# Softcap attention and routed experts in one kernel: a fixed order for all engines, row-split scores, two expert slots

## The chip, the core and the metric

One core of a Trainium2 chip. TensorE (PE in the profile) multiplies, ScalarE (ACT) evaluates tanh and exp, VectorE (DVE) and GpSimd (POOL) do the rest of the element work, SyncE (SP) issues most transfers. The metric is device time in microseconds, the median over runs of the same program.

## What is computed

```python
def _attn_ref(q, k, v, cap):                 # 8 batches, 12 heads, 448 tokens, 64 wide
    scores = q @ k^T / sqrt(64)
    scores = cap * np.tanh(scores / cap)     # cap = 30
    scores = scores - max(scores)
    attn = exp(scores) / (sum(exp(scores)) + 1e-9)
    return attn @ v

def _moe_ref(x, w_gate, wq, wk, wv, wo):     # x: 8 x 448 x 768, 4 experts of 64
    logits = x @ w_gate
    topk = the two largest; w = softmax over those two
    for e in range(4):
        q, k, v = x @ wq[e], x @ wk[e], x @ wv[e]
        a = causal softmax of (q @ k^T / sqrt(64))
        ye = a @ v @ wo[e]
        out += (w of e where e is among the token's two, else 0) * ye
    return out
```

The second stage reads the first stage's output with the heads side by side.

## The kernel before

Stage A runs over 48 pairs of heads (`NP`; six to a batch, `HP`). A pair's scores are held transposed, keys on the 128 partitions. The 448 keys of a head are cut into three chunks of 128 and 64 that remain; the remainders of the two heads share one tile `kt`. The chunks of head 0 and head 1 lie in the upper and lower 64 rows of `kz`, with zeros in the other half, so each of the six score products (and the seventh with `kt`) contracts over all 128 rows. `fill` writes them into tiles `s` of two banks (`ps_score`, two tiles); `tanh` reads each tile (three of 896 elements a row, one of 448), `expo` runs once for each head (1792 and 1344 elements), with no maximum subtracted, since the cap bounds the scores. `a_pv_mm` multiplies by the values with a column of ones beside them, which gives the sum; `a_pv_out` divides, `a_xt` transposes into `xT`. `a_tr` transposes q and k through PE into one bank and VectorE copies them out in five pieces (`qt` twice, `kz` twice, `kt`). The casts to f16 run on GpSimd (`a_cast`), four pairs ahead.

Stage B follows batch by batch, while the next batch's pairs run: `b_v` (values of four experts and the gate's logits), `b_qk` (projections, two experts a half `r`), `b_gate` and `b_gexp` (top two and weights), `b_fill` and `b_exp` (scores and exponentials of each expert, causal: 1024 and 960 elements a half, two halves), `b_pv` for each of four experts, `b_ot`, `b_wo`, `b_out`. GpSimd sets the future positions to zero with 16 `affine_select` a batch. The last batch has no pairs to hide behind; `last_batch` writes out its order.

PSUM has eight banks: four for scores, four (`ps_aux`, tiles `tps`, `pv`, `xtp`, `vps`, ...) shared by all else. The order of each queue is settled when the program is built: ScalarE's list `prog` is written out, and class `Plan` places PE work between the score fills by modelled durations and due times, with VectorE following PE. `slot` issues loads (a pair of pairs each, five stage buffers), and up to three weight loads a pair on GpSimd's queue; outputs leave on SP.

Of the kernel before, what the change touches and what calls it, by code (L numbers as in the profile page):

```python
# [13 lines left out]


class Plan:

    LAT = 0.2

    def __init__(self):
        self.pe = self.dve = self.act = 0.0
        self.done = {}
        self.aux = [0.0] * 4
        self.naux = 0
        self.opened = {}
        self.work = []  # L30

    def ready(self, u):
        t = 0.0
        for d in u["deps"]:
            if d not in self.done:
                return None
            t = max(t, self.done[d])
        if u["aux"] in ("open", "whole"):
            t = max(t, self.aux[self.naux % 4])
        return t  # L40

    def emit(self, u):
        start = max(self.pe, self.ready(u))
        u["fn"]()
        self.pe = start + u["pe"]
        end = self.pe + self.LAT
        if u["dve"]:
            self.dve = max(self.dve, end) + u["dve"]
            end = self.dve + self.LAT
        if u["aux"] in ("open", "whole"):  # L50
            slot = self.naux % 4
            self.naux += 1
            self.aux[slot] = end
            if u["aux"] == "open":
                self.aux[slot] = 1.0e9
                self.opened[u["group"]] = slot
        self.done[u["key"]] = end
        if u["aux"] == "close":
            self.aux[self.opened.pop(u["group"])] = end
            self.done[u["group"]] = end  # L60

    def step(self, until, latest):


        at = {}
        for u in self.work:
            r = self.ready(u)
            if r is not None:
                at[u["key"]] = max(r, self.pe)
        if not at:  # L70
            return False
        first = min(at.values())
        u = min(
            (u for u in self.work if at.get(u["key"], 1.0e9) <= first + 0.05),
            key=lambda u: u["due"],
        )
        if first > until or first + u["pe"] > latest:
            return False
        self.work.remove(u)
        self.emit(u)  # L80
        return True

    def pump(self, until, latest):
        while self.pe < until and self.step(until, latest):
            pass

    def known(self, key):
        return key in self.done or any(key in (u["key"], u["group"]) for u in self.work)

    def force(self, key):  # L90


        def hurry(k):
            for u in self.work:
                if k in (u["key"], u["group"]):
                    u["due"] -= 1.0e6
                    for d in u["deps"]:
                        hurry(d)

        hurry(key)  # L100
        while key not in self.done:
            assert self.step(1.0e9, 1.0e9), key

    def add(self, key, pe, dve, deps, due, fn, *args, aux="whole", group=None):


        self.work.append(
            dict(
                key=key, pe=pe, dve=dve, deps=deps, due=due, fn=lambda: fn(*args), aux=aux,
                group=group,  # L110
            )
        )

    def parts(self, key, n, pe, dve, deps, due, fn, *args):

        for i in range(n):
            d = deps if i == 0 else [(*key, "part", i - 1)]
            aux = "open" if i == 0 else "close" if i == n - 1 else None
            self.add(
                (*key, "part", i), pe / n, dve * (i == n - 1), d, due, fn, *args, i, aux=aux,  # L120
                group=key,
            )
# [3 lines left out]
def kernel(  # L126
# [25 lines left out]
    TL = S - KM  # L152

    WIN = (0, 128, 256, S - 128)

    const = ctx.enter_context(tc.tile_pool(name="const", bufs=1))
    stage = ctx.enter_context(tc.tile_pool(name="stage", bufs=5))
    hd = ctx.enter_context(tc.tile_pool(name="hd", bufs=3))
    actp = ctx.enter_context(tc.tile_pool(name="actp", bufs=3))
    xp = ctx.enter_context(tc.tile_pool(name="xp", bufs=2))  # L160
    bp = ctx.enter_context(tc.tile_pool(name="bp", bufs=2))
    outp = ctx.enter_context(tc.tile_pool(name="outp", bufs=4))
    ps_score = ctx.enter_context(
        tc.tile_pool(name="ps_score", bufs=2, space=bass.MemoryType.PSUM)
    )
    ps_aux = ctx.enter_context(tc.tile_pool(name="ps_aux", bufs=4, space=bass.MemoryType.PSUM))

    ctx.enter_context(tc.manual_schedule())


    staged = {}

    def load(p, n=2):

        if p >= NP:
            return
        b, j = divmod(p, HP)
        h0, h1 = 2 * j, 2 * (j + n)
        e2 = nc.scalar if n == 1 else nc.sync
        qf = stage.tile([QP, 2 * n, QC * Dh], f32, name=f"qf_{p}", tag="qf")  # L180
        kf = stage.tile([128, 2 * n, KC * Dh], f32, name=f"kf_{p}", tag="kf")
        vf = stage.tile([128, 2 * n, KC * Dh], f32, name=f"vf_{p}", tag="vf")
        ktf = stage.tile([128, n, Dh], f32, name=f"ktf_{p}", tag="ktf")
        vtf = stage.tile([128, n, Dh], f32, name=f"vtf_{p}", tag="vtf")

        def tails(dst, src):
            t = src[b, h0:h1, KM:S].rearrange("(j two) p d -> two p j d", two=2)
            nc.sync.dma_start(dst[0:64], t[0])
            e2.dma_start(dst[64:128], t[1])

        e2.dma_start(qf, q[b, h0:h1].rearrange("h (p c) d -> p h (c d)", c=QC))
        nc.sync.dma_start(kf, k[b, h0:h1, 0:KM].rearrange("h (p c) d -> p h (c d)", c=KC))
        tails(ktf, k)
        later = [
            lambda: nc.sync.dma_start(
                vf, v[b, h0:h1, 0:KM].rearrange("h (p c) d -> p h (c d)", c=KC)
            ),
            lambda: tails(vtf, v),
        ]
        if n == 2:  # L200
            for f in later:
                f()
        for i in range(n):
            h = slice(2 * i, 2 * i + 2)
            staged[p + i] = (qf[:, h], kf[:, h], vf[:, h], ktf[:, i], vtf[:, i])
        return later

    LOAD, CAST, TR = 8, 4, 2
    for f in load(0, 1) + load(1, 1):
        f()  # L210


    warm = const.tile([128, 512], f16, name="warm")
    nc.vector.memset(warm, 0.0)
    ident = const.tile([128, 128], f16, name="ident")
    make_identity(nc, ident)
    kz = [const.tile([128, 2, KM], f16, name=f"kz{i}") for i in range(4)]
    ktz = [const.tile([128, 128], f16, name=f"ktz{i}") for i in range(6)]
    for t in (ktz[0], kz[0], ktz[1], kz[1]):
        nc.vector.memset(t, 0.0)  # L220

    def evac(dst, src, act=False):
        (nc.scalar.copy if act else nc.vector.tensor_copy)(dst, src)  # L223


    cast = {}
    vcast = {}

    def a_cast(p, eng=None):
        if p >= NP:  # L230
            return
        eng = nc.gpsimd if eng is None else eng
        if 2 <= p < len(ktz):
            nc.gpsimd.memset(ktz[p], 0.0)
        if 2 <= p < len(kz):
            nc.gpsimd.memset(kz[p], 0.0)
        assert p < 8 or ("pv", p - 8, 1) in plan.done and ("tr", p - 6) in plan.done
        qf, kf, vf, ktf, vtf = staged.pop(p)
        q16 = hd.tile([QP, QC, 2, Dh], f16, name=f"q16_{p}", tag="q16", bufs=6)
        k16 = hd.tile([128, KC, 2, Dh], f16, name=f"k16_{p}", tag="k16", bufs=6)  # L240
        eng.tensor_copy(q16, qf.rearrange("p h (c d) -> p c h d", c=QC))  # L241
        nc.gpsimd.tensor_copy(k16, kf.rearrange("p h (c d) -> p c h d", c=KC))  # L242
        for g in range(2):
            r = slice(64 * g, 64 * (g + 1))
            eng.tensor_copy(ktz[p % 6][r, r], ktf[r, :])
        cast[p] = (q16, k16)
        vcast[p] = (vf, vtf)
        if p > 1:
            a_castv(p)

    def a_castv(p):
        vf, vtf = vcast.pop(p)
        if p < len(v16):
            nc.gpsimd.memset(v16[p][:, :, :, Dh : Dh + 1], 1.0)
            nc.gpsimd.memset(vtz[p], 0.0)
            for g in range(2):
                nc.gpsimd.memset(vtz[p][64 * g : 64 * (g + 1), g, Dh : Dh + 1], 1.0)
# [47 lines left out]
    def fill(p, i):  # L305
        qt, kk, kt = qkt[p]
        if i == 3:
            del qkt[p]
# [23 lines left out]

    xt = {}

    pvs = {}

    def a_pv_mm(p, i, n, heads):

# [632 lines left out]
```

## Time and profile before

| | us |
|---|---|
| median of three runs (340.18 to 342.02) | 341.12 |
| profiled execution: span from first to last instruction, its own time | 341.0 |
| ScalarE busy | 308.4 |
| PE busy (modelled ends) | 280.2 |
| VectorE busy | 251.1 |
| GpSimd busy | 165.2 |

The granted TensorE clock was 0.989 of full speed on average. In rows of groups, the columns are line, engine, operation, output<-input, shapes and count, then busy us and mean ns of one, then idle time of the engine just before and what ended it. In rows of the timeline and of the chain the first two numbers are start and length in us; a merged row ("x2") covers several instructions. In rows of windows, the stretch comes first, its length, then busy us of PE, PE's weight loads, VectorE, ScalarE and GpSimd, each with its count.

### The profile page before, as it was taken

To read this page: it belongs to the slowest core of one execution; us is meant where nothing else is said; L and a number is where in the kernel's file an instruction comes from. 1 tells how busy PE (TensorE), PEld (TensorE's weight loads), DVE (VectorE), ACT (ScalarE), POOL (GpSimd) and SP (SyncE) were. 2 spreads that over 40 slices of the span, in tenths; PEclk is the share of its full clock that TensorE was granted. 3 is DMA by queue.
4 is the path that set the end of the run, shared out by engine and by line. 5 is a ranking of instruction groups with operands and counts; after the bars stand their busy time and mean duration, and the time that the engine had idled before them with its cause. 6 is when DMAs were issued, how large, how long until landed. Compare 5 with 4: busy or idle time off the path is not lost.

```text
span 341.0 us, 8954 instructions
## 1 busy us (share of the span) xinstructions
PE 280.2 (82%) x3295; PEld 190.1 (56%) x3295; DVE 251.1 (74%) x877; ACT 308.4 (90%) x341; POOL 165.2 (48%) x527
## 2 busy tenths in 40 slices
PE   5766669697899789998799879997899789979772
PEld 1344346465457565765576655765576566657441
DVE  2456656378767897869977897889887897788673
ACT  1999999689999999999999999999999999995422
POOL 2889999555806293256707291438506430220130
PEclk9999999799999999999999999999999999999997
DMA  5989999860172915392087606490162001210116
GB/s 160 264 222 244 244 223 241 202 173 3 48 208 72 293 32 171 123 289 71 7 253 211 184 2 187 138 303 24 47 210 72 3 2 46 94 24 2 48 54 226
DMA packets 65148, 46.21 MB, mean 136 GB/s; under 512 B 25872, under 2 KB 61584, under 8 KB 65104
## 3 DMA queue, kind: packets, MB, share of 16 engines
q1 hardware_dynamic: 53712, 43.43, 44.4%
q0 software_dynamic: 10512, 1.58, 7.3%
q10 hardware_dynamic: 880, 0.62, 0.6%
q8 instruction: 26, 0.43, 0.5%
q14 instruction: 18, 0.15, 0.1%
HBM read 36.19 MB, written 11.01 MB: 138 GB/s over the span
## 4 chain that ended last, share of the span: by engine, by line
ACT 85%; PE 6%; DMA 2%; issue 2%; DVE 2%; POOL 1%; ACTq 0%; POOLq 0%
ACT y L323 39%; ACT p L330 37%; ACT pB L540 7%; POOL pB L548 1%; DMA kf<-in_k_dram 1%; PE qkps L469 1%; PE vps L407 1%; PE s L312 1%; DMA out_dram<-ob 1%; PE sB L528 1%; DMA vtf<-in_v_dram 1%; DVE ob L223 1%; PE qps L469 0%; PE pv L351 0%; ACT L223 0%
## 5 line engine op out<-in xcount | busy, mean ns | idle before, releaser
L323 ACT ACTIVATE y<-s 128x896 f16<-128x896 f32 x192 | 152.6, 880 | 1.9 <-PE s L312 1.9
L330 ACT ACTIVATE p<-y 128x1792 f16<-128x1792 f16 x96 | 149.6, 1562 | 0.0
L548 POOL TENSOR_SCALAR_AFFINE_SELECT pB<-pB 128x128 f16<-128x128 f16 (+1 forms) x128 | 31.9, 280 | 142.9 <-ACT pB L540 141.7
L312 PE MATMUL s<-qt,kz 128*128 128x448 f16 x288 | 82.0, 357 | 14.0 <-ACT y L323 6.0
L351 PE MATMUL pv<-v,p 128*128 128x65 f16 x1152 | 66.2, 194 | 1.2 <-ACT p L330 1.0
L351 PEld LDWEIGHTS <-p 128*128 128x128 f16 x1152 | 53.7, 98 | 11.0 <-ACT p L330 2.0
L346 PE MATMUL pv<-vtz,p 128*128 128x130 f16 x192 | 42.0, 220 | 3.1 <-DVE kz L223 3.0
L364 DVE TENSOR_TENSOR xk<-pv,rc 128x256 f16<-128x256 f32 x96 | 40.7, 424 | 3.3
L312 PEld LDWEIGHTS <-kz 128*128 128x128 f16 x288 | 26.2, 98 | 26.4 <-issue 13.1
L223 DVE COPY ob<-wops 128x384 f32<-128x384 f32 (+1 forms) x60 | 33.1, 556 | 9.3 <-PE wops L594 8.5
L540 ACT ACTIVATE pB<-sB 128x1024 f16<-128x1024 f32 (+1 forms) x32 | 31.9, 999 | 2.4 <-PE sB L528 2.4
L223 DVE COPY kz<-tps 64x384 f16<-64x384 f16 x94 | 32.9, 350 | 0.7
L379 PE MATMUL xtp<-perm,xk 128*128 128x128 f16 x144 | 21.0, 223 | 14.4 <-DVE xk L364 14.2
L594 PE MATMUL wops<-wo,oT 128*128 128x384 f16 x128 | 29.8, 325 | 1.7 <-DVE oT L588 1.7
L407 PE MATMUL vps<-wvg,xT 128*128 128x260 f16 (+1 forms) x192 | 30.6, 276 | 0.0
L379 PEld LDWEIGHTS <-xk 128*128 128x128 f16 x192 | 14.6, 98 | 27.3 <-DVE xk L364 19.1
L363 DVE RECIPROCAL rc<-pv 128x4 f32<-128x4 f32 x96 | 17.2, 179 | 16.6 <-PE pv L351 15.4
L241 POOL CAST q<-qf 112x512 f16<-112x512 f32 x46 | 28.2, 613 | 2.0
L289 DVE COPY qt<-tps 128x384 f16<-128x384 f16 x48 | 16.9, 352 | 15.2 <-PE tps L279 14.8
L242 POOL CAST k<-kf 128x384 f16<-128x384 f32 x48 | 24.4, 509 | 5.0 <-DMA kf<-in_k_dram 5.0
L390 DVE COPY xT<-xtp 128x448 f16<-128x448 f16 x48 | 18.6, 388 | 11.2 <-PE xtp L379 10.8
L258 POOL CAST v<-vf 128x384 f16<-128x384 f32 x48 | 24.4, 508 | 3.5 <-DMA vf<-in_v_dram 0.5
(100 smaller groups left out, 500.5 us busy)
## 6 DMA issues: line engine op xcount, KB each, us to landing
qf<-in_q_dram SPq DMA_DIRECT2D x23, 448.0 KB, 5.2
out_dram<-ob SPq DMA_DIRECT2D x24, 384.0 KB, 2.8
kf<-in_k_dram SPq DMA_DIRECT2D x23, 384.0 KB, 5.3
vf<-in_v_dram SPq DMA_DIRECT2D x23, 384.0 KB, 4.6
ktf<-in_k_dram SPq DMA_DIRECT2D x46, 32.0 KB, 4.7
vtf<-in_v_dram SPq DMA_DIRECT2D x46, 32.0 KB, 4.1
out_dram<-ob SPq DMA_DIRECT2D x7, 192.0 KB, 2.8
qf<-in_q_dram ACTq DMA_DIRECT2D x2, 224.0 KB, 4.1
```

The lines of the kernel that those rows point to most:

```text
L223: (nc.scalar.copy if act else nc.vector.tensor_copy)(dst, src)
L312: nc.tensor.matmul(sc[:, o, 0:S], lhsT, qt, start=True, stop=True)
L323: nc.scalar.activation(y[(p, g)][:, 2 * (i % 2) : 2 * (i % 2) + n, :], score.pop((p, i))[:, 0:n, 0:S], AF.Tanh, scale=isc / capf,)
L330: nc.scalar.activation(pt, y.pop((p, g)), AF.Exp, scale=capf)
L346: nc.tensor.matmul(pv[:, n, :, :], pt[:, KC, w : w + 128], vtz[p % 8], start=(n == 0), stop=False, skip_group_check=True,)
L351: nc.tensor.matmul(pv[:, n, g, :], pt[:, c, w : w + 128], v16[p % 8][:, g, c, :], start=False, stop=(c == KC - 1), skip_group_check=True,)
L364: nc.vector.tensor_tensor(xt[p][:, 2 * i : 2 * i + 2, :, :], pv[:, :, :, 0:Dh], rc.broadcast_to((128, 2, 2, Dh)), ALU.mult,)
L379: nc.tensor.transpose(ps[:, 128 * n : 128 * (n + 1)], src(n), first if n < 3 else last)
L407: nc.tensor.matmul(ps, xT[b][:, j, w : w + 128], wvg[:, j, 0:cols], start=(j == 0), stop=(j == NDC - 1),)
L540: nc.scalar.activation(pb[:, o0 : o0 + n], st[b].pop(("sc", r, g))[:, 0:n], AF.Exp, scale=isc)
L548: nc.gpsimd.affine_select(out=blk, in_=blk, compare_op=ALU.is_ge, fill=0.0, base=0, pattern=[[1, n]], channel_multiplier=-1,)
L594: nc.tensor.matmul(ps, st[b]["oT", r][:, w : w + 128], wo2[r][:, f * (D // 2) : (f + 1) * (D // 2)], start=(r == 0), stop=(r == 1),)
```

## The change

All of the program but the launch is rewritten. Every instruction is declared with its engine, an assumed occupancy and latency, what it reads and writes, and its group of one bank; `Graph.solve` then places them one at a time, on all five engines, by readiness and due time, three times over, and emits the order found. ScalarE's tanh and exponentials keep the order in which they are declared.

- Scores: `fill` keeps the two heads of a pair in the two halves of 64 rows, without zeros; the two products of a chunk go to two banks from different rows. Only the remainders use all rows.
- Banks: X has three (chunk 0 of both heads, remainders), Y two (chunks 1 and 2 in turn), three are left for all else (A0 to A2). Groups of the second stage can borrow X banks while they are idle.
- ScalarE: tanh of 1344, 896 and 896 elements, and one exponential of 3136 in place for a pair. Its order is X, first Y, the pair before's exponential, then second Y.
- Second stage of seven batches: two slots (first and second choice of each token) instead of four experts. `b_mask` spreads each slot's 0/1 choice over the 64 columns on GpSimd, PE transposes it, VectorE multiplies it into q; `b_score` accumulates both halves of experts, so each query meets the keys of its expert alone; `b_pv` multiplies by the values of all four experts (260 columns) and the mask with the weight picks one; `b_ot` adds both slots while transposing. The gate ranks experts by pairwise comparison and needs the exponential of one difference a token.
- The last batch keeps four experts, with row-split scores, 512-wide exponentials and its values in two banks.
- `tr` is copied out by one instruction of 960 elements; casts go to rings of three; four stage buffers for loads; weights are loaded from the start on GpSimd's queue; a small exponential draws the table load ahead; the first pair begins with a Y chunk.

```diff
-class Plan:
...
+class Graph:
...
+    def solve(self, banks, lent):
...
-        sc = ps_score.tile([128, 2, 512], f32, name=f"s{i}_{p}", tag="score")
-        for o, (g, c) in enumerate(HALF[i]):
-            lhsT = kt if c == KC else kk[:, g, 128 * c : 128 * (c + 1)]
-            nc.tensor.matmul(sc[:, o, 0:S], lhsT, qt, start=True, stop=True)
+        def heads():
+            for g in range(2):
+                r = slice(64 * g, 64 * (g + 1))
+                nc.tensor.matmul(
+                    dst[:, g, 0:S], qk[t][r, S + 128 * (c + 1) : S + 128 * (c + 2)],
+                    qk[t][r, 0:S], start=True, stop=True,
+                )
...
+        if what == "X":
+            pe(S, lambda: nc.tensor.matmul(
+                X[:, 2, 0:S], qk[t][:, S : S + 128], qk[t][:, 0:S], start=True, stop=True),
+                rd, [("s", bs[2])], name=f"sT_{p}", takes=bs[2:3])
...
+        ACTS[what, p] = act(c_act(S * (b - a)), lambda: nc.scalar.activation(
+            y[:, a:b, :], src[:, 0 : b - a, 0:S], AF.Tanh, scale=isc / capf),
...
+            act(c_act(S * (b - a), False), lambda a=a, b=b: nc.scalar.activation(
+                y[:, a:b, :], y[:, a:b, :], AF.Exp, scale=capf), ks, ks, fixed=True,
+                name=f"e{p}")
...
+        dve(c_dve(S + 512, True),
+            lambda: nc.vector.tensor_copy(qk[t], bank16(g)[:, 0 : S + 512]),
...
+    def b_mask(b, s):
...
+            nc.gpsimd.tensor_copy(
+                mB[s], ms[s][x].rearrange("p n (e o) -> p n e o", o=1).broadcast_to((128, 4, E, Dh))
+            )
...
+            dve(c_dve(S, True), lambda g=g, r=r: nc.vector.tensor_tensor(
+                qm[s][r], qB[x][r], bank16(g)[:, 0:S], ALU.mult),
...
+    H0 = ((0, KC, KM, 64), (64, 0, 0, 128), (192, 1, 128, 128), (320, 2, 256, 128),
+          (448, 2, KM, 64))
+    H1 = ((512, 0, 128, 320), (832, 1, 256, 192))
...
+                    for r in range(2):
+                        nc.tensor.matmul(
+                            ps[:, o % 512 : o % 512 + n], kB[x][r][:, keys(c)],
+                            qm[s][r][:, q0 : q0 + n], start=(r == 0), stop=(r == 1),
+                        )
...
+        act(c_act(1024), lambda: nc.scalar.activation(
+            pb[:, 64:], X[:, 0:2, :].rearrange("p a c -> p (a c)"), AF.Exp, scale=isc),
+            [("s", "X0"), ("s", "X1")], [("pB", pi)], fixed=True, name=f"eB{b}_{s}",
+            frees=("X0", "X1"))
...
+                        nc.tensor.matmul(
+                            bank(g)[:, 0 : E * (Dh + 1)], pB[pi][:, o : o + 128],
+                            vB[x][:, c, :, :], start=(t == 0), stop=(t == len(cs) - 1),
+                        )
...
+            dve(c_dve(E * Dh), lambda g=g, k_=k_, n=n: nc.vector.scalar_tensor_tensor(
+                oB[s][:, n, :, :], view(g)[:, :, 0:Dh], rcb[k_][:, 0, :],
+                mw[s][x][:, n, :].rearrange("p (e o) -> p e o", o=1).broadcast_to((128, E, Dh)),
+                ALU.mult, ALU.mult),
...
+    act(1.3, lambda: nc.scalar.activation(rcb[0], warm[:, 0:4].rearrange("p (n o) -> p n o", o=1),
+                                          AF.Exp), ["warm"], [("rcb", 0)])
+    load(0, 1)
+    load(1, 1)
+    weights()
...
+        order = ("Y1", "X", "Y2") if p == 0 else ("X", "Y1", "Y2")
+        for what in order:
+            if what == "Y2" and p:
+                expo(p - 1)
+                if p in exps:
+                    b_score(*exps[p])
...
+            fill(p, what)
+            tanh(p, what)
...
+    for _ in range(3):
+        G.dues(when)
+        order = G.solve(AUX, XB + YB)
+        when = {o.idx: o.start for o in fixed}
+    for o in order:
+        o.fn()
```

More of the change, by code (lines that the diff above doesn't have):

```diff
@@ L13 @@
 AX = mybir.AxisListType
-class Plan:
-    LAT = 0.2
-    def __init__(self):
[L25 to L62, printed above, removed]
-        at = {}
[L66 to L122, printed above, removed]
@@ L125, with c_pe, c_dve, c_act @@
+def c_pe(n):
+    return max(n / 2400.0 + 0.002, 0.029)
+def c_dve(n, half=False):
+    return n / 1920.0 + 0.064 if half else n / 960.0 + 0.073
+def c_act(n, psum=True):
+    return n / 1200.0 + (0.05 if psum else 0.093)
+def c_pool(n):
+    return n / 1000.0 + 0.07
 @with_exitstack
@@ L208 @@
[L208 to L223, printed above, removed]
@@ L226 @@
[L226 to L242, printed above, removed]
+    LB = B - 1
@@ new lines, with bank, bank16, pe @@
+    for i in range(3):
+        BANK[f"X{i}"] = X[:, i, :]
+    for i in range(2):
+        BANK[f"Y{i}"] = Y[:, i, :]
+    XB = tuple(f"X{i}" for i in range(3))
+    YB = tuple(f"Y{i}" for i in range(2))
+    ANY = AUX + XB + YB
+    def bank(g):
+        return BANK[g.bank]
+    def bank16(g):
+        return BANK[g.bank].bitcast(f16)
+    def pe(n, fn, r=(), w=(), grp=None, due=None, name="", occ=None, takes=()):
+        occ = c_pe(n) if occ is None else occ
+        return G.op("PE", occ, fn, r, w, occ + 0.165, due, grp, name=name, takes=takes)
@@ new lines, with gate @@
+    wo2 = [sb(f"wo2_{r}", [128, D]) for r in range(2)]
+    wvg = sb("wvg", [128, NDC, E * Dh + E])
+    ident = sb("ident", [128, 128])
+    perm = sb("perm", [128, 128])
+    pswap = sb("pswap", [128, 128])
+    swap = sb("swap", [128, 128])
+    warm = sb("warm", [128, 512])
+    tri = sb("tri", [128, 4, E, E], f32)
+    rank0 = sb("rank0", [128, 4, E], f32)
+    rank1 = sb("rank1", [128, 4, E], f32)
+    def gate(nm, shape):
+        return [sb(f"{nm}{i}", shape, f32) for i in range(2)]
+    g_c = gate("g_c", [128, 4, E, E])
@@ new lines @@
+    expo(NP - 1, (("X", "Y1"), ("Y2",)))
+    pv(NP - 1)
+    xt(NP - 1, (ACTS["Y2", NP - 1], 4.0))
+    last(ACTS["Y2", NP - 1], 9.0)
+    for o in G.ops:
+        o.first = o.name[:2] in ("sX", "sY", "sT", "tr", "qk", "k1", "q1", "ge")
+    fixed = [o for o in G.ops if o.eng == "ACT" and o.fixed]
+    when, t = {}, T0
+    for o in fixed:
+        when[o.idx] = t
+        t += o.occ
+    for _ in range(3):
+        G.dues(when)
+        order = G.solve(AUX, XB + YB)
+        when = {o.idx: o.start for o in fixed}
```

1473 lines of the change are left out of this document (840 added, 633 removed).

## The prediction

> **What bounds the kernel now.** I read the page's busy table and chain of waits first, to see which engine the end hangs on, then the costliest groups for the counts, then windows over one stretch of six pairs and over the tail.
>
> ```profile
> span 341.0 us, 8954 instructions
> PE 280.2 (82%) x3295; PEld 190.1 (56%) x3295; DVE 251.1 (74%) x877; ACT 308.4 (90%) x341; POOL 165.2 (48%) x527
> ACT 85%; PE 6%; DMA 2%; issue 2%; DVE 2%; POOL 1%; ACTq 0%; POOLq 0%
> L323 ACT ACTIVATE y<-s 128x896 f16<-128x896 f32 x192 | 152.6, 880 | 1.9 <-PE s L312 1.9
> L330 ACT ACTIVATE p<-y 128x1792 f16<-128x1792 f16 x96 | 149.6, 1562 | 0.0
> 102.20:139.80 37.60, 33.47 (x403) 23.24 (x403) 31.34 (x108) 37.60 (x43) 18.44 (x59) 1.00 0.50 148
> ```
>
> The columns of the last row are PE, PEld, DVE, ACT and POOL busy time, then the granted clock. ScalarE does not rest once in 37.6 us, six pairs plus one batch of the second stage, while PE is busy 33.5 us (89%) and VectorE 31.3 (83%). 85% of the chain is ScalarE. The rest of the span is a start before the first tanh, one stall, and a tail:
>
> ```profile
> 9.73 1.73 ACT L323 ACTIVATE y<-s 128x896 f16<-128x896 f32 x2 [0.26 <-PE s L312]
> 64.22 0.91 PE L469 MATMUL qps<-xT,wq 128*128 128x448 f16 x2 [2.69 <-issue]
> 65.96 0.97 ACT L540 ACTIVATE pB<-sB 128x960 f16<-128x960 f32 x1 [2.39 <-PE sB L528]
> 310.60:317.80 7.20, 7.16 (x101) 5.03 (x102) 4.75 (x15) 1.18 (x2) 0.00 (x0) 1.00 0.01 2
> 317.80:321.80 4.00, 1.63 (x13) 0.93 (x12) 2.78 (x9) 2.12 (x6) 0.00 (x0) 1.00 0.25 98
> 321.80:326.00 4.20, 4.09 (x44) 3.27 (x44) 1.90 (x10) 4.16 (x6) 2.96 (x13) 1.00 0.00 0
> 326.00:336.00 10.00, 6.15 (x65) 3.67 (x62) 8.56 (x24) 1.80 (x4) 0.98 (x4) 1.00 0.35 122
> 336.00:341.00 5.00, 0.00 (x0) 0.00 (x0) 0.00 (x0) 0.00 (x0) 0.00 (x0) 0.62 0.68 233
> ```
>
> **The tanh and exp of the pairs.** Durations overlap their neighbours, so starts are what counts:
>
> ```profile
> 33.06 1.33 ACT L330 ACTIVATE p<-y 128x1344 f16<-128x1344 f16 x1
> 34.27 1.36 ACT L323 ACTIVATE y<-s 128x896 f16<-128x896 f32 x2
> 35.52 1.70 ACT L330 ACTIVATE p<-y 128x1792 f16<-128x1792 f16 x1
> 37.10 1.73 ACT L323 ACTIVATE y<-s 128x896 f16<-128x896 f32 x2
> 38.70 1.35 ACT L330 ACTIVATE p<-y 128x1344 f16<-128x1344 f16 x1
> ```
>
> A pair takes 38.70 - 33.06 = 5.64 us. The exponentials start 1.21 and 1.58 us ahead of what follows, so 448 elements cost 0.37 us (0.83 ns each) and a start 0.09. Two tanh of 896 take 1.60, so a tanh start costs about 0.06. The elements of a pair stay (7 x 448). One of four tanh starts and one of two exp starts go: 0.15 us a pair, 48 pairs, **-7.2 us**; a pair becomes 5.49.
>
> **The second stage's exponentials.** A batch had four (1024 and 960 wide), it gets two of 1024:
>
> ```profile
> 61.32 1.04 ACT L540 ACTIVATE pB<-sB 128x1024 f16<-128x1024 f32 x1
> 62.24 1.33 ACT L330 ACTIVATE p<-y 128x1344 f16<-128x1344 f16 x1
> ```
>
> One of 1024 occupies 0.92 us, one of 960 by the slope 0.87. 3.58 becomes 1.84, 1.74 saved in each of the seven batches ahead of the last, **-12.2 us**. Six pairs with a batch then need 6 x 5.49 + 1.84 + 0.1 (gate) = 34.9 us of ScalarE; the same sum for the kernel before gives 37.5, where the window shows 37.6.
>
> **Whether PE still fits.**
>
> ```profile
> 38.54 0.54 PE L312 MATMUL s<-qt,kz 128*128 128x448 f16 x2
> L312 PE MATMUL s<-qt,kz 128*128 128x448 f16 x288 | 82.0, 357 | 14.0 <-ACT y L323 6.0 <-ACT pB L540 3.1 <-ACT kz L223 2.4
> 59.87 0.49 PE L407 MATMUL vps<-wvg,xT 128*128 128x260 f16 x3
> 59.45 0.33 PE L279 MATMUL tps<-ident,k 128*128 128x128 f16 x3
> ```
>
> Two scores of 448 columns take 0.54 and one is recorded as 0.35, so they follow each other by 0.19 us, 0.42 ns a column (transposes of 128 and products of 260 fit that). A pair had seven; it now has three couples (each head in its own 64 rows, its own bank) and one full one. If the two of a couple run together, that is four slots, 3 x 0.19 x 6 = -3.4 us a batch; if one after the other, 0. No row shows such a couple. I take together, as they share neither operand rows nor banks, and keep both ends. Per batch the second stage adds, by columns: 16 mask transposes of 128 (+0.9), 20 products of 260 columns for 40 of 65 (+0.9), 16 instead of 8 transposes of outputs (+0.4), scores 4096 columns for 3968 (+0.1): +2.3. PE comes to 33.5 - 3.4 + 2.3 = 32.4 of 34.9, 93%, against 89% that left ScalarE no idle time. The waits are roomier too: two-bank scores were refilled under one tanh (0.80); now the first Y is refilled under the X tanh (0.83 x 1344 + 0.06 = 1.18) and the second under the 2.7 us exponential.
>
> **VectorE and GpSimd.**
>
> ```profile
> L223 DVE COPY kz<-tps 64x384 f16<-64x384 f16 x94 | 32.9, 350 | 0.7
> L390 DVE COPY xT<-xtp 128x448 f16<-128x448 f16 x48 | 18.6, 388 | 11.2 <-PE xtp L379 10.8
> L289 DVE COPY qt<-tps 128x384 f16<-128x384 f16 x48 | 16.9, 352 | 15.2 <-PE tps L279 14.8
> L293 DVE COPY qt<-tps 128x64 f16<-128x64 f16 x48 | 8.6, 180 | 0.0
> L296 DVE COPY kt<-tps 128x128 f16<-128x128 f16 x48 | 9.9, 206 | 1.9 <-ACT kz L223 1.9
> ```
>
> Five copies (352 + 180 + 2 x 350 + 206 = 1438 ns) become one of 960 elements, by the slope from 128 to 448 about 680: -4.6 us a batch. The batch part grows: 16 gate operations for 9 (+1.3, by the 180 ns of the smallest copy), four mask products (+1.6 by the 388 ns of the copy of that size, up to twice that), eight scaled outputs for four (+1.6 likewise), less 1.5 for four copies of second-stage keys that go. Together about -1.6, up to nothing: 30 to 31 of 34.9 us, 85 to 90% (83% before). It stays hidden, with less cover. GpSimd drops no pair casts, trades 16 masks a batch for four and gains two spreads of 1024; at 18.4 us it has room.
>
> **What the new order adds on ScalarE.** Two waits. The X banks are lent to the second stage: after its exponential the next X scores must be written under one tanh, 0.80 us, and a couple needs 0.19 to issue, 0.35 to land and two handovers of up to 0.26 (the idle time ahead of the first tanh above): 0 to 0.4 over, 0.2 taken, 14 times, +2.8. And the gate's exponential, fixed in ScalarE's order, waits for eleven small VectorE steps where it waited for the logits alone: at about 0.2 us a step 0 to 2.2, seven times; it stands where the planner expects them done, so I take 0.5, +3.5. Behind it on ScalarE stand the tanh, and behind those PE's refills. **+6.3 us** (0 to 15).
>
> **The stall at 62 us.** PE waited 2.69 us ahead of the first `wq` product of the second half.
>
> ```profile
> kf<-in_k_dram SPq DMA_DIRECT2D x23, 384.0 KB, 5.3
> ...
> wq<-in_moe_wq_dram POOLq DMA_DIRECT2D x4, 96.0 KB, 12.2
> q0 software_dynamic: 10512, 1.58, 7.3%
> ```
>
> That queue's loads land 12.2 us after issue in the median. They are now issued at the start instead of three a pair, so ScalarE's 2.39 us go: **-2.4** (0 to -2.8). In return seven of them stand on GpSimd's queue ahead of the first cast of pair 2, and their packets (7.3% of 341 us, 25 us of all 16 engines for 17 loads, 1.5 a load) share the DMA with the loads of pairs 0 to 3. On SP the stores now stand between the loads, and one that waits for its copy holds those behind it; as the stage holds eight pairs and the casts run three ahead, a load has five pairs, 27 us, for its 5.3 to land. I cost that at nothing; a store over 20 us late would uncover it.
>
> **The start.**
>
> ```profile
> 6.94 1.28 ACT L223 ACT_TABLE_LOAD   x1 [6.94 <-DMA vtf<-in_v_dram]
> 8.24 0.47 ACT L223 COPY kz<-tps 64x384 f16<-64x384 f16 x1
> ```
>
> The table load (1.28, on the path) is drawn ahead by a dummy exponential, and one copy of keys replaces two of 0.47, so the first tanh comes near 9.73 - 1.28 - 0.47 = 8.0. But PE's queue has the transposes of pair 2 ahead of the X scores of pair 1; pair 2 must have landed by about 9.5, and its loads share the DMA with the weights: 0 to 3 us late. Net -1.5 to +1.5, **-0.5** taken.
>
> **The tail.**
>
> ```profile
> 327.47 0.43 DVE osc L578
> 327.95 0.41 PE otp L379 x4
> 328.38 0.40 DVE oT L588
> ...
> 329.33 0.32 PE pvB L570 x10
> ```
> ```profile
> 332.99 2.12 PE L594 MATMUL wops<-wo,oT 128*128 128x384 f16 x12 [1.51 <-DVE oT L588]
> ```
>
> Before, by the windows, PE works 7.2 us on end (projections of the last batch that lagged), then come 4.0 of evacuations in turn, 4.2 of exponentials, 10 to the last copy, 5.0 to the end. The new order leaves PE some 20 slots of 0.19 (projections, four output products) behind the last exponential, 3.8; the values' 24 products of 256 (0.11 each, 2.6), under which the evacuations run; eight exponentials of 512 (8 x 0.49 = 3.9); one pass of products, scaling, transposes and copies (0.32 + 0.43 + 0.41 + 0.40, a second scaling and the small steps: 2.6); 2.9 for the output products as before, from 332.99 to 335.9; and 5.0: together 20.8 against 30.4. PE may arrive 1 to 2 us behind. **-8** (-5 to -9.5).
>
> **Sum**, against the profiled execution's 341.0 (the median of three is 341.12): 341.0 - 7.2 - 12.2 + 6.3 - 2.4 - 0.5 - 8 = **317.0 us**.
>
> **The rivals.**
>
> *PE becomes the bound.* The array empties when it passes between 64-row and full products: six passages a pair, each between 0 and the 0.16 us by which a record outlasts the spacing (0.35 - 0.19). At 0.08 a batch gains 2.9 us, PE needs 35.3, just over ScalarE's 34.9; at 0.16, 38.3, seven times 3.4 more. For it: PE is at 93% in my sum. Against: records overlap, so 93% overstates, and the order places other work around the couples. Time 322 to 341, 330 in the middle. The Trainium skill, "TensorEngine Tiling (Array Packing)", section "Key Properties", states this rule: changing the tiling mode drains TensorE. No row here has a mode change, so the trace neither bears it out nor denies it.
>
> *Three work banks instead of four, and one fixed order for all engines.* VectorE, near 87%, frees banks late, PE waits for them, and fills come late: 0.2 us a pair, 10 us in all. For it: VectorE's share grows while the banks that hide its delays shrink. Against: the idle score banks are lent out, and the transposed pairs run up to four ahead. 327.
>
> *Slower: the couples run one after the other and each passage empties the array.* 32.4 + 3.4 + 2.9 to 5.9 = 38.7 to 41.7 us of PE per batch, PE is late in each refill, 7 x 3.8 or more: 317 + 27 = 344, up to 365. It outweighs all the gains once PE needs over 34.9 + 24/7 = 38.3 us a batch. Against: it takes both prices near their upper ends. The Trainium skill, "TensorE: Matmul & The Clock Gate", Part 3, says products in distinct row groups run at the same time; by it this rival falls back to the first. Nothing in this trace shows it.
>
> **How the numbers follow.** Forecast 0.58 (its own range 309 to 324); PE as the bound 0.16, of which 0.03 ends within 0.5% of before; banks and order 0.12; slower 0.14. So faster by over 0.5% 0.83, within 0.5% (about what a measurement of this kernel can tell from none) 0.03, slower 0.14. The low end is all gains at their bounds without waits, near 309; the high end, 333, takes in the second rival and the lower half of the first and leaves the slower one out.
>
> **What would show it.** ScalarE without idle time over six pairs, about 35 us a batch; 144 tanh, 49 pair exponentials, 14 of the second stage; the two score products of a couple starting within 0.02 us; PE near 32 us a batch; no wait at the first `wq` product; first tanh near 8 us; some 22 us behind the last exponential. Wrong if ScalarE waits for X or Y scores more than 0.2 us a pair, if the couples start 0.19 apart, or if score products follow others with 0.1 us or more of silence.

## The result, and the profile after

The changed kernel takes 337.09 us (median of 20 runs, 336.0 to 340.42) against 340.24 us of the kernel before (338.99 to 342.52): a ratio of 0.9913, with an interval of 0.9891 to 0.9935. Faster by a little under 1%; the forecast was 317.0. The profiled execution spans 334.4 us, against 341.0 before, and the reading below goes by it: 17.4 us are missing. (The 341.0 is a long execution of the kernel before: those measured beside the experiments span 336.5 to 340.9. So the difference of the two spans overstates the gain, and the ratio is what counts for that.)

The page of the changed kernel, its busy table, its chain of waits and the groups that answer to those of before:

```profile
span 334.4 us, 8992 instructions
PE 293.5 (88%) x3435; PEld 193.5 (58%) x3435; DVE 239.2 (72%) x752; ACT 291.7 (87%) x232; POOL 160.6 (48%) x451
PE 56%; DVE 17%; POOL 7%; DMA 6%; issue 5%; ACT 5%; SPq 1%; ACTq 0%; DVEq 0%; POOLq 0%
L587 ACT ACTIVATE yp<-yp 128x3136 f16<-128x3136 f16 (+2 forms) x49 | 135.7, 2772 | 0.0
L577 ACT ACTIVATE yp<-Y 128x896 f16<-128x896 f32 x96 | 88.8, 925 | 10.0 <-PE Y L555 9.2
L577 ACT ACTIVATE yp<-X 128x1344 f16<-128x1344 f32 x48 | 62.5, 1302 | 3.7 <-PE X L555 2.2
```

The counts are as announced (96 + 48 tanh, 49 exponentials of pairs), and ScalarE is busy 291.7 us for 308.4. But the chain, 85% ScalarE before, is now 56% PE and 5% ScalarE. Windows of the changed kernel, first over six pairs with one batch of the second stage, then over the tail (columns as in the prediction's windows, and behind the granted clock the share of the DMA engines and GB/s):

```profile
136.74:173.66 36.92, 34.97 (x433) 23.94 (x430) 29.98 (x95) 35.39 (x29) 18.02 (x49) 1.00 0.54 151
309.25:314.70 5.45, 5.45 (x67) 3.71 (x66) 3.94 (x11) 0.00 (x0) 0.00 (x0) 1.00 0.20 75
314.70:319.24 4.54, 3.20 (x35) 2.42 (x34) 3.33 (x13) 1.07 (x3) 0.00 (x0) 1.00 0.22 87
319.24:324.30 5.06, 3.53 (x54) 1.95 (x53) 4.24 (x19) 4.31 (x9) 2.96 (x8) 1.00 0.29 97
324.30:330.45 6.15, 4.15 (x36) 2.28 (x33) 4.63 (x14) 1.92 (x5) 0.00 (x0) 1.00 0.33 112
330.45:334.40 3.95, 0.00 (x0) 0.00 (x0) 0.00 (x0) 0.00 (x0) 0.00 (x0) 1.00 0.65 203
```

PE is busy 35.0 us in a batch where the forecast had 32.4. PE's timeline in the changed kernel (start, duration, line, operation, how many) shows what a couple costs:

```profile
139.48 0.36 PE L555 MATMUL Y<-qk 64*128 64x448 f16 x2
139.68 0.35 PE L555 MATMUL X<-qk 64*128 64x448 f16 x2
139.96 0.50 PE L903 MATMUL A<-wo,oT 128*128 128x384 f16 x2
...
142.56 0.34 PE L607 MATMUL A<-v,yp 128*128 128x65 f16 x6
142.83 0.36 PE L555 MATMUL Y<-qk 64*128 64x448 f16 x2
143.12 0.23 PE L600 MATMUL A<-vtz,yp 128*128 128x130 f16 x1
143.19 0.35 PE L607 MATMUL A<-v,yp 128*128 128x65 f16 x6
143.38 0.22 PE L600 MATMUL A<-vtz,yp 128*128 128x130 f16 x1
```

The two products of a couple are one row of 0.36 us, as long as a single one: they run together. Two couples side by side start 0.20 apart. But the full product behind a couple starts 0.28 or 0.29 after it, 0.09 more; and ahead of the couple, where six products of 65 columns take 0.19 (143.19 to 143.38) and so end at 142.75, PE starts nothing until 142.83. The same shows in the whole trace: from a full product of 448 columns to the next full one it is 0.19 us, to a couple behind it 0.285 in the median, and from a couple to a full product 0.29. A lone couple therefore holds PE for 0.19 + 2 x 0.09 = 0.37 us, which is what two full products cost (0.38). With 139 stretches of split products in PE's order, of 144 couples, that is 139 x 0.18 = 25 us of PE in the whole span.

ScalarE's waits in the changed kernel (engine and line, what it waited for, us in total, times, longest):

```profile
ACT yp L577 <- PE Y L555: 9.2, 16, 2.0
...
ACT g_e L731 <- DVE g_e L726: 4.2, 6, 1.3
...
ACT yp L577 <- PE X L555: 2.2, 4, 0.8
```

### The profile page after: what moved, and what is told of

Read it like the earlier page. It is cut to its first block, busy times and chain, and to the rows that moved or that the text cites. A ratio compares the mean times of both kernels' runs of the same rounds, so it can differ in the third digit from the quotient of the medians.

```text
span 334.4 us, 8992 instructions
## 1 busy us (share of the span) xinstructions
PE 293.5 (88%) x3435; PEld 193.5 (58%) x3435; DVE 239.2 (72%) x752; ACT 291.7 (87%) x232; POOL 160.6 (48%) x451
## 4 chain that ended last, share of the span: by engine, by line
PE 56%; DVE 17%; POOL 7%; DMA 6%; issue 5%; ACT 5%; SPq 1%; ACTq 0%; DVEq 0%; POOLq 0%
PE A L607 7%; PE A L686 7%; PE A L662 6%; PE Y L555 5%; PE A L903 5%; PE A L600 4%; DVE oB L865 3%; PE A L641 3%; DMA ktf<-in_k_dram 3%; PE X L792 3%; PE X L564 3%; PE A L850 2%; ACT yp L577 2%; PE X L555 2%; DVE oT L888 2%
## 5 line engine op out<-in xcount | busy, mean ns | idle before, releaser
L587 ACT ACTIVATE yp<-yp 128x3136 f16<-128x3136 f16 (+2 forms) x49 | 135.7, 2772 | 0.0
L577 ACT ACTIVATE yp<-Y 128x896 f16<-128x896 f32 x96 | 88.8, 925 | 10.0 <-PE Y L555 9.2
L577 ACT ACTIVATE yp<-X 128x1344 f16<-128x1344 f32 x48 | 62.5, 1302 | 3.7 <-PE X L555 2.2
L607 PE MATMUL A<-v,yp 128*128 128x65 f16 x1152 | 58.1, 197 | 0.0
L607 PEld LDWEIGHTS <-yp 128*128 128x128 f16 x1152 | 51.7, 100 | 4.6 <-issue 3.0
L600 PE MATMUL A<-vtz,yp 128*128 128x130 f16 x192 | 43.2, 226 | 6.6 <-ACT yp L587 3.0
L629 DVE TENSOR_TENSOR xk<-A,rca 128x256 f16<-128x256 f32 x96 | 40.5, 423 | 2.7
L544 DVE COPY qk<-A 128x960 f16<-128x960 f16 x47 | 29.6, 650 | 11.7 <-PE A L513 11.4
L555 PE MATMUL Y<-qk 64*128 64x448 f16 x192 | 36.2, 373 | 0.7 <-ACT yp L577 0.5
L912 DVE COPY ob<-A 128x384 f32<-128x384 f32 (+1 forms) x55 | 29.3, 552 | 3.2 <-PE A L903 2.4
L600 PEld LDWEIGHTS <-yp 128*128 128x128 f16 x192 | 18.9, 99 | 15.2 <-issue 9.3
L523 PE MATMUL A<-ident,k 128*128 128x128 f16 x144 | 16.9, 229 | 10.5 <-POOL k L485 7.1
```

The source lines that it names most:

```text
L544: lambda: nc.vector.tensor_copy(qk[t], bank16(g)[:, 0 : S + 512]),
L555: nc.tensor.matmul(dst[:, g, 0:S], qk[t][r, S + 128 * (c + 1) : S + 128 * (c + 2)], qk[t][r, 0:S], start=True, stop=True,)
L577: ACTS[what, p] = act(c_act(S * (b - a)), lambda: nc.scalar.activation(y[:, a:b, :], src[:, 0 : b - a, 0:S], AF.Tanh, scale=isc / capf), [ ...
L587: act(c_act(S * (b - a), False), lambda a=a, b=b: nc.scalar.activation(y[:, a:b, :], y[:, a:b, :], AF.Exp, scale=capf), ks, ks, fixed=True ...
L600: nc.tensor.matmul(ps[:, n, :, :], y[:, 2, w : w + 128], vtz[u], start=(n == 0), stop=False, skip_group_check=True,)
L607: nc.tensor.matmul(ps[:, n, h, :], y[:, SLOT[c][h], w : w + 128], v16[u][:, h, c, :], start=False, stop=(c == 2), skip_group_check=True,)
```

## Experiments

Theory P: passages between split and full products cost about 0.09 us each and make PE the bound. Rival O: a couple costs its 0.19, and the time is lost to the order and to the three work banks.

**Undo the split, or half of a couple.** The three edits are in the loop that sends a couple:

```diff
# e1_two_full
-                r = slice(64 * g, 64 * (g + 1))
+                r = slice(0, 128)
# e2_one_full (e3_one_half keeps r as it was)
-            for g in range(2):
-                r = slice(64 * g, 64 * (g + 1))
+            one = what != "X" and p >= 2
+            for g in range(1 if one else 2):
+                r = slice(0, 128) if one else slice(64 * g, 64 * (g + 1))
```

> The changed kernel with both products of each couple over all 128 rows, so no passage between 64-row and full products is left; the two heads' scores are summed, the output is not the reference's. Theory P (passages): a couple now holds PE for 0.19 + 2 x 0.09 = 0.37 us, two full products for 0.38: time unchanged within 1% (334 to 339 us), PE busy near 293 us, no silence ahead of the score products. Rival O (couples cost 0.19 as forecast; the lost time comes from the order and the three work banks): 18 couples a batch cost 0.19 more each, 3.4 us a batch, 24 us in all: near 360 us.

> The changed kernel with each Y couple (12 a batch, from pair 2 on) cut to one product over all 128 rows; the second Y bank keeps old scores, the output is not the reference's. The X couples stay split. Theory P: PE loses 12 x 0.18 = 2.2 us a batch, and as PE sets the pace the pairs speed up until ScalarE's 35.3 us a batch bind: 11 us less or somewhat more, 322 to 328 us, ScalarE's waits for Y scores (9.2 us) mostly gone. Rival O: less than 3 us gained, 333 to 337 us.

> As e2_one_full, but the one product left of each Y couple is over 64 rows, so both passages stay and only the second product goes; the second head's scores of the Y banks are left out. Theory P: the two products of a couple do run together and the price is that of the passages: time as the changed kernel's, 333 to 339 us. Rival (the second product of a couple costs PE a slot of its own): like e2_one_full, 322 to 328 us.

Measured: e1 335.93 us, ratio to before 0.9906 (0.9876 to 0.9937), the changed kernel's own; e2 329.43, 0.9712 (0.9688 to 0.9736); e3 336.97, 0.9946 (0.9914 to 0.9978). The same place in PE's timeline, of e1, e3 and e2 in turn:

```profile
142.56 0.54 PE L555 MATMUL Y<-qk 128*128 128x448 f16 x2
142.93 0.22 PE L600 MATMUL A<-vtz,yp 128*128 128x130 f16 x1
```
```profile
142.08 0.36 PE L556 MATMUL Y<-qk 64*128 64x448 f16 x1
142.37 0.23 PE L601 MATMUL A<-vtz,yp 128*128 128x130 f16 x1
```
```profile
139.13 0.35 PE L556 MATMUL Y<-qk 128*128 128x448 f16 x1
139.32 0.22 PE L601 MATMUL A<-vtz,yp 128*128 128x130 f16 x1
```

Two full products hold PE for 0.37, one split product alone for 0.29 and the silence ahead of it, one full product for 0.19. The second product of a couple is free, the passages are not, and splitting the rows gained PE nothing. Rival O's 360 us for e1 is out. e2 gained 7.5 us by the spans (326.9 against 334.4) where 11 or somewhat more were expected; its span lies in the 322 to 328 us named, its median above. ScalarE's waits for Y scores fell from 9.2 us to 6.3, of which 4.6 stand in the first six pairs. The smaller gain says that passages aren't all.

**The planner's prices.** e4 tells the planner of passages, e7 gives a lone couple its measured price and moves other numbers of the plan.

```diff
# e4_plan_state
+PASS = 0.09
...
+        def cross(o):
+            return PASS if o.eng == "PE" and split(o) != was[0] else 0.0
...
-            return t
+            return t + cross(o)
...
-    ... occ=0.22, name=f"s{what}_{p}"
+    ... occ=0.19, name=f"s{what}_{p}"
# e7_replan
-                    d = u.due if u.first else max(u.due, t0 + 0.8)
+                    d = u.due if u.first else max(u.due, t0 + 0.4)
...
-    ... u.due < t + o.occ + 0.6 and t2 < t + min(o.occ, 0.25) ...
+    ... u.due < t + o.occ + 0.4 and t2 < t + min(o.occ, 0.15) ...
...
-    ... occ=0.22, name=f"s{what}_{p}"
+    ... occ=0.37, name=f"s{what}_{p}"
...
-    ... due=(ref, 7.0 + 1.4 * n)
+    ... due=(ref, 10.0 + 1.4 * n)
...
-    ... due=(ref, 12.0 + 3.6 * r + ...)
+    ... due=(ref, 16.0 + 3.6 * r + ...)
...
-            [(b, "m1"), (b, "m2")], ["e"])
+            [(b, "m1"), (b, "m2")], ["e"], lat=0.9)
```

> The full computation. Only the planner's idea of PE changes: a couple costs 0.19, and 0.09 more stands wherever PE goes from split to full products or back, so the planner sets couples side by side where it can: 117 episodes of split products instead of 139. Theory P: 22 x 0.18 = 4 us of PE go, and the plan's times come nearer to the chip's: 329 to 334 us. Rival O: 335 to 339 us, unchanged.

> The full computation. Only numbers of the planner change: a couple 0.37 for 0.22, the gate's last step 0.9 us late for 0.2, second-stage products due 3 to 4 us later, closer look-ahead. Theory P with an order made on wrong prices: PE's work stays, but the score products stand where they are needed and ScalarE's waits for Y, X and second-stage scores (about 14 us) fall by 5 or more: 327 to 331 us. Rival: any other order loses as much elsewhere, as in e4_plan_state: 334 to 341 us.

Measured: e4 342.56 us, 1.0115 (1.0081 to 1.015), slower than both kernels and outside both ranges expected; e7 331.07, 0.974 (0.9703 to 0.9777), by its span of 328.8 what theory P expected. e4 has fewer passages and loses far more in single places. ScalarE and PE in e4 at one of them:

```profile
202.02 2.93 ACT L597 ACTIVATE yp<-yp 128x3136 f16<-128x3136 f16 x1
207.56 0.92 ACT L587 ACTIVATE yp<-Y 128x896 f16<-128x896 f32 x1 [2.60 <-PE Y L565]
```
```profile
204.38 1.05 PE L672 MATMUL A<-wvg,xT 128*128 128x260 f16 x8
...
207.15 0.36 PE L565 MATMUL Y<-qk 64*128 64x448 f16 x2
```

The exponential ends at 204.95, but the second stage's value products and other work stand ahead of the Y couple in PE's order, which is sent at 207.15. So the order does matter, in both directions: part of rival O holds beside P. And right prices alone don't make a good order: e4's 0.19 and two passages of 0.09 are what a lone couple was measured to cost. That both changes are needed shows in the next run.

**Both together.**

```diff
# e10_replan_one: e7_replan, with the loop of e2_one_full
```

> The kernel of e7_replan, same order, with each Y couple from pair 2 on cut to one product over 128 rows (second head's Y scores left out, as in e2_one_full). Under the better order a batch takes 36.3 us where ScalarE's own work is 35. If passages are what is left, PE's 2.2 us a batch bring it to 35 to 35.5 us and the time to 321 to 325 us. If e7_replan is held by its order and no longer by PE's work, 326 to 329 us.

Measured: 324.36 us, 0.953 (0.949 to 0.9571), span 322.1. The X tanh of pairs 6 and 42 (six batches apart), as ScalarE's timeline has them in the changed kernel, e2, e7 and e10:

```profile
42.95 1.32 ACT L577 ACTIVATE yp<-X 128x1344 f16<-128x1344 f32 x1
...
267.13 1.34 ACT L577 ACTIVATE yp<-X 128x1344 f16<-128x1344 f32 x1
```
```profile
42.92 1.35 ACT L578 ACTIVATE yp<-X 128x1344 f16<-128x1344 f32 x1
...
260.42 1.34 ACT L578 ACTIVATE yp<-X 128x1344 f16<-128x1344 f32 x1
```
```profile
44.56 1.32 ACT L577 ACTIVATE yp<-X 128x1344 f16<-128x1344 f32 x1
...
262.13 1.32 ACT L577 ACTIVATE yp<-X 128x1344 f16<-128x1344 f32 x1
```
```profile
44.14 1.32 ACT L578 ACTIVATE yp<-X 128x1344 f16<-128x1344 f32 x1
...
255.02 1.33 ACT L578 ACTIVATE yp<-X 128x1344 f16<-128x1344 f32 x1
```

A sixth of each difference is the length of a batch:

| us per batch | order of the change | order of e7 |
|---|---|---|
| all couples split | 37.36 | 36.26 |
| Y couples one full product | 36.25 | 35.15 |

The two changes add: 1.1 us a batch each. With both, a batch stands at 35.15, beside the 34.9 forecast for ScalarE alone. What in e7's order gains its 1.1 is only in part known: between the two tanh, ScalarE's waits for the gate's exponential go from 3.0 us to none and those for Y scores from 4.4 to 1.1, while those for second-stage scores rise from 0.5 to 3.0; which of the plan's numbers did it was not separated. The window of e10 over one batch shows the bound back on ScalarE, which does not rest in it, nor in four of the six batches between the two tanh:

```profile
143.06:177.97 34.91, 33.07 (x417) 23.76 (x416) 29.60 (x95) 34.91 (x29) 18.13 (x48) 1.00 0.57 159
```

Over the whole span, start and tail included, e10's chain still has 50% PE and 21% ScalarE.

**The gate's exponential.** In the gate, the largest logit is taken off first and the last step becomes a maximum:

```diff
# e5_gate
...
+            g_l[x], lg[x], g_m1[x].broadcast_to((128, 4, E)), ALU.subtract),
...
-    ... g_l[x], ms[0][x], -1.0e30, lg[x], ALU.mult, ALU.add
+    ... g_l[x], ms[0][x], -1.0e30, g_l[x], ALU.mult, ALU.add
...
-        g_(lambda: V.reduce_max(g_m2[x], g_l[x], axis=AX.X), ...
-        g_(lambda: V.tensor_tensor(g_e[x], g_m2[x], g_m1[x], ALU.subtract), ...
+        g_(lambda: V.reduce_max(g_e[x], g_l[x], axis=AX.X), ...
```

> The full computation. The gate takes the largest logit off ahead of the ranks and ends in a maximum, so that no small VectorE operation with two operands in SBUF is left between the masks (which start GpSimd's 1024-element spread) and the gate's exponential. Theory L: the 4-element subtraction took 0.53 to 0.85 us in five of seven batches because it ended with the spread that ran beside it; with it gone ScalarE's waits ahead of the gate's exponential fall from 4.2 us to under 1. Rival: VectorE's backlog is what is late, and the 4.2 us stay. For the time, theory P (PE sets the pace) lets at most 2 us of that come through: 332 to 335 us in the profiled execution; if ScalarE set the pace, 330 to 331.

Measured: 336.41 us, 0.9905 (0.987 to 0.9939): no change that can be told. VectorE beside GpSimd in the changed kernel, then in e5:

```profile
172.57 0.17 DVE L725 TENSOR_REDUCE g_m<-g_l 128x4 f32<-128x16 f32 x1
172.78 0.74 DVE L726 TENSOR_TENSOR g_e<-g_m,g_m 128x4 f32<-128x4 f32 x1
```
```profile
172.46 2.03 POOL L753 CAST mB<-ms 128x1024 f16<-128x1024 f32 x2 [2.50 <-DVE ms L720]
```
```profile
172.83 0.17 DVE L728 TENSOR_REDUCE g_e<-g_l 128x4 f32<-128x16 f32 x1
```
```profile
172.72 2.03 POOL L754 CAST mB<-ms 128x1024 f16<-128x1024 f32 x2 [2.50 <-DVE ms L720]
```

The subtraction ends at 173.52, when the first of the two spreads ends (172.46 + 1.04); the maximum in e5 runs beside a spread in 0.17. The mechanism of theory L is seen, but not what it was to explain: ScalarE still waited 3.8 us for the gate, where theory L had less than 1, so the rival holds. The wait most likely comes from where the exponential stands in ScalarE's order, too early for a VectorE that runs late: in e7, where the plan counts on 0.9 us for that step, the wait is gone with the old gate, though e7 moves other numbers too.

**The weight loads.** e6 issues them behind the casts of pair 3; e11 is e7 with them spread over the pairs 1 to 11.

```diff
# e6_weights_late
-    gp(0.85, lambda: nc.gpsimd.dma_start(dst, src), w=[key], ...
+    gp(0.85, lambda: nc.gpsimd.dma_start(dst, src), [("q16", 3 % NQ16)], [key], ...
...
     load(1, 1)
-    weights()
...
         cast(p)
+        if p == 3:
+            weights()
# e11_replan_spread
+        AT = [1, 1, 2, 2, 3, 3, 4, 4, 5, 5, 6, 6, 6, 8, 9, 10, 11]
...
+            if AT.pop(0) == p:
...
+        weights(p)
```

> The full computation. The 17 weight loads are issued behind the casts of pair 3 instead of at the start. Theory S: their packets hold back the loads of pairs 0 to 3, which cost the first batch ScalarE waits of 3.7 us behind the first tanh: these fall under 1.5, and the time to 331 to 333 us. Rival: those loads fill the DMA engines by themselves, or the stall comes back at the first products with the weights near 45 to 62 us: 334 to 338 us.

> The full computation: the kernel of e7_replan, with the same order on PE, and the weight loads spread out, one to three with the casts of each of the pairs 1 to 11 instead of all at the start. Theory S: ScalarE's waits in the first 46 us (e7_replan: 7.3 us) shrink by 2 us or more without a stall behind it: 325 to 327 us. Rival: the DMA engines are full for 45 us either way, and what is gained at the first pairs is lost at the next, as in e6_weights_late: 328 to 330 us.

Measured: e6 337.48 us, 0.9935 (0.9895 to 0.9975); e11 330.76, 0.9717 (0.9664 to 0.9771), which can't be told from e7. Theory S was half right, and the times are what its rivals expected (e11's by its span of 328.3). In e6 ScalarE's waits in the first 24 us shrink (0.32 and 0.66 us behind the first tanh, where the changed kernel had 0.59, 2.00 and 0.83) and come back 20 us later, on its timeline:

```profile
19.31 0.92 ACT L577 ACTIVATE yp<-Y 128x896 f16<-128x896 f32 x1 [0.66 <-PE Y L555]
41.27 0.92 ACT L577 ACTIVATE yp<-Y 128x896 f16<-128x896 f32 x1 [1.66 <-PE Y L555]
44.75 0.92 ACT L577 ACTIVATE yp<-Y 128x896 f16<-128x896 f32 x1 [1.39 <-PE Y L555]
```
```profile
34.63 0.52 POOL L455 DMA_DIRECT2D wo<-in_moe_wo_dram  x1 [1.45 <-DMA wq<-in_moe_wq_dram]
```

The second fence is GpSimd in e6: issuing a load, it waits, by the profile, for an earlier one of its own queue to land, and the casts of the next pairs stand behind it. That is not all of it: PE starts nothing in the 1.8 us before 33.99, and in the windows from 34 to 44 us its granted clock is 0.50 to 0.52, where a couple's row is 0.56 us long for 0.36. How much of the two stalls is the clock's wasn't separated.

**Versions with everything.** e8 is e5's gate, e6's loads and e4's planner with later due times and another look-ahead; e9 is e5's gate and a planner that knows passages too, with other numbers (couple 0.22, passage 0.06) and without the late loads; e12 is e5's gate and prices near e7's, and sends a pair's second Y couple together with the next pair's X couple.

```diff
# e12_merged
+            def both():
+                heads()
+                for g in range(2):
+                    r = slice(64 * g, 64 * (g + 1))
+                    nc.tensor.matmul(X[:, g, 0:S], qk[u][r, S + 128 : S + 256], qk[u][r, 0:S], ...
```

> The full computation: the gate of e5_gate, the late weight loads of e6_weights_late, and a planner that knows a couple as 0.19 and each passage as 0.09 with the later due times. 114 episodes of split products for 139, 4.5 us less of PE. If the parts add up: 323 to 328 us. If the order decides by chance, as in e4_plan_state: 333 to 340 us.

> The full computation: the gate of e5_gate, the weights loaded at the start as in the changed kernel, and a planner that counts each passage (a couple 0.22, a passage 0.06) with second-stage products due later: 115 episodes of split products. e8_all lost 5.4 us in one stall at 42 us behind its late weights; without it theory P gives 327 to 330 us. If setting couples side by side is no use, as e4_plan_state could be read, 332 us or more.

> The full computation: the gate of e5_gate, and the second Y couple of a pair sent as one operation with the X couple of the next pair (33 times, wherever no second-stage scores stand between), so that 110 episodes of split products are left of 139; prices in the planner as in e7_replan (a lone couple 0.40, a double one 0.50). Theory P: against e7_replan 28 x 0.18 = 5 us less of PE's work; if half of it comes through, 326 to 329 us. If, as in e9_aware_gate, the new order gives back what the passages save: 330 to 334 us.

Measured: e8 333.46 us, 0.9822 (0.9779 to 0.9865); e9 331.96, 0.9752 (0.9703 to 0.98); e12 330.32, 0.9721 (0.9661 to 0.9781). By their medians all three missed what theory P gave for them, e12 narrowly: e8 and e12 lie in their rival's range, e9 just below it (e12's span, 327.5, would be theory P's). Their 110 to 115 stretches of split products instead of 139 save 4 to 5 us of PE, yet e9 and e12 end where e7 ends with 138, and e8 above it: what setting couples side by side brings wasn't separated from what the new order costs. Between the X tanh of pairs 6 and 42, e12's batches take 35.71 us each (45.06 to 259.29), 0.56 less than e7's, and the rest of its span gives 2 of these 3.3 us back; e8's and e9's batches, 36.5 and 36.6, are no shorter than e7's. The fastest versions that compute everything are e7, e11 and e12, at 0.972 to 0.974 of the kernel before and below the changed kernel's interval; e9, at 0.975, can't be told from them.

## Why the prediction was wrong

Of the 17.4 us between 317.0 and 334.4, 9.4 lie between the X tanh of pairs 6 and 42 (224.2 us, where six batches of 34.9 and 0.9 of waits make 214.8), 3.0 at the start, 2.8 in the tail, and what is left, 2.2, by subtraction on the last six pairs, where ScalarE waits 3.6 us for 0.9 counted.

- **ScalarE's savings: right.** A pair that waits for nothing takes 5.47 us (forecast 5.49), a second-stage exponential 0.91 (0.92), and four of e10's batches, at 34.86 to 34.96 with ScalarE busy throughout, are the forecast 34.9.
- **PE: the step that failed.** "I take together" was right, and "That is four slots, 3 x 0.19 x 6 = -3.4 us a batch" was not: a couple costs 0.37 with its passages, so -3.4 became about 0, and PE had 35.0 us of work a batch for 32.4 (the couples alone would make it 35.8, so its other terms came out 0.8 smaller together). The first rival named this mechanism, its price within 0.01 us, PE's 35.3 and a range of 322 to 341, and got a chance of 0.16. By its own rule, though, 0.09 a passage makes 32.4 + 36 x 0.09 = 35.6 us of PE and a time near 322: that 334.4 lies in its range is in part luck. The row for a passage was missing, and the sum took it at zero although the bound was 0 to 0.16 six times a pair. Of its own signs of being wrong, the silence of 0.09 stayed just under the 0.1 it named, and the waits for X and Y scores behind the first tanh (10.3 us over 48 pairs, 0.21 a pair) just passed its 0.2. The Trainium skill, "TensorEngine Tiling (Array Packing)", section "Key Properties", has TensorE drain at a change of tiling mode: the trace agrees, 0.09 us each way. The Trainium skill, "TensorE: Matmul & The Clock Gate", Part 3, has products in distinct row groups run at the same time: e3 agrees.
- **The new waits: the two that it named came out, a third was put at nothing.** +6.3 us was taken, 0.9 a batch. The gate's exponential waits 4.2 us for 3.5, and X scores behind a second-stage exponential 2.2 for 2.8. But "The waits are roomier too" failed: between the X tanh of pairs 6 and 42 ScalarE waits 4.4 us for Y scores, 10 times out of 12 for a first Y couple behind an X tanh. In all a batch is 37.36 there where ScalarE needs 34.8, so 2.6. e2, e7 and e10 divide it: 1.1 for the Y couples' passages, 1.1 for the order, 0.35 left. "The order places other work around the couples" was the argument against the first rival; with two engines at 35 us of work each, the order's share came out as large as that of the Y couples' passages.
- **The stall at 62 us: right.** No wait stands ahead of a `wq` product there.
- **The start: mis-sized.** The first tanh comes at 8.52 (forecast 8.0), but ScalarE then waits 3.7 us in the first six pairs where 1.2 was counted. e6 moves these waits rather than removing them.
- **The tail: mis-sized.** 25.2 us instead of 22.4 (30.4 - 8), by the windows: PE works 5.4 us behind the last exponential (3.8 and 1 to 2 late), evacuations with the values' products take 4.5 (2.6), the exponentials 5.1 (3.9), and the 10.1 behind them agree with 10.5.
- **Banks (the second rival):** not tried alone; e10 keeps the three banks, and only 0.35 us a batch is left there. **The slower rival** needed couples that run in turn, and e3 shows that they don't.
- **Slips in the sums** that decide nothing: 20 products of 260 columns for 40 of 65 are +1.1 us by columns, not +0.9; the terms named for the lent X banks reach 0.26 over, not 0.4; and the upper bounds of the two waits, 0.4 x 14 and 2.2 x 7, make 21, not 15.

## What to carry to other kernels

A row split saves TensorE time only if the passages are few beside the split products: here two 64-row products with full ones on both sides cost as much as two full products. When a change takes work off the bounding engine and leaves a second one within a tenth of it, the next bound is the question, and an unpriced cost on that second engine must enter the forecast at its middle and not at zero. With two engines near the bound, the order of the work is a cost of its own: another order of the same work (e7, with other prices, due times and look-ahead) was worth as much as the Y couples' passages. Measured prices alone didn't find it: e4 had them and was slower than both kernels.

## What the runs showed of the hardware

A passage between 64-row and full products costs PE 0.09 us each way. A VectorE subtraction of four elements with both operands in SBUF takes 0.16 us where no cast runs (in the last batch) and up to 0.85 beside a GpSimd cast, ending when the cast does, while a maximum with one operand takes 0.16 to 0.17 beside the same casts (e5). The Trainium skill, "SBUF — State Buffer", section "Who interferes with whom", has the instruction with two SBUF inputs contend with a GpSimd one that reads SBUF, and the one with a single input not; these rows agree. A DMA issue on GpSimd's queue waited up to 2.4 us, by the profile for an earlier load of that queue to land, as this row of GpSimd's timeline in e8 shows, with the casts behind it:

```profile
39.20 0.52 POOL L465 DMA_DIRECT2D wo<-in_moe_wo_dram  x1 [2.44 <-DMA wk<-in_moe_wk_dram]
```
